# Four tokens on each partition, one batch on each 32 partitions, heads in two halves, in an RWKV attention with a soft mixture of experts

## The chip, the cores and the metric

One core of one Trainium2 chip. The metric is the time of one execution in microseconds of the device, the median of several runs. A run called slow here is over 1.5% above the fastest run of the same kernel; ratios use the other runs alone. A profile shows one execution. TensorE multiplies matrices, VectorE and ScalarE work element by element, GpSimd does too and also issues the DMA of the weights; SyncE issues the other DMA transfers.

## The reference

```python
# r, k, v: [B=4, H=8, S=768, D=48]   w (decay), u (bonus): [8, 48]   float32
for t in range(S):
    cur   = einsum('bhd,bhe->bhde', u * k[t], v[t])
    y[t]  = einsum('bhd,bhde->bhe', r[t], state + cur)
    state = w * state + einsum('bhd,bhe->bhde', k[t], v[t])
x = y.transpose(0, 2, 1, 3).reshape(3072, 384)          # tokens x model
logits = x @ phi                                        # phi: [384, 32], 8 experts of 4 slots
d = softmax(logits, over tokens); c = softmax(logits, over slots)
slot_in  = d.T @ x
slot_out = relu(slot_in[e] @ w1[e]) @ w2[e]             # per expert, F = 1024
return c @ slot_out                                     # [3072, 384]
```

Both kernels work in chunks of 128 tokens: within a chunk the scores k·r are masked by order and multiplied with v ("intra"), what came before is a state of 48 x 48 per head ("inter"), and decay is put into r and k beforehand by tables `W_n` and `W_k`. The loop has 12 steps in either kernel, of 256 tokens x 384 columns before and of 512 tokens x 192 columns after. Routing (transposes, logits, exponentials, dispatch sums) runs a step or two behind. Then come the expert matmuls and an output stage that writes 4.7 MB.

## The kernel before

A step is 256 tokens of one batch, two tokens on each of 128 partitions; all eight heads at once. So a chunk lies on 64 partitions, and a step's two chunks follow each other through one state.

```python
    def load(n):                                  # three transfers of 393 KB a step, 384-byte pieces
        b, i = divmod(n, nSb)
        for x, src in ((1, k), (0, r), (2, v)):
            nc.sync.dma_start(out=t[:].rearrange("p h j d -> p h (j d)"),
                              in_=src[b, :, i * TS:(i + 1) * TS, :].rearrange("h (p j) d -> p h (j d)", j=J))
    ...
    # att(n, j): 16 score matmuls (32 a step), 64x64 tiles; then two masking multiplies on VectorE
    nc.tensor.matmul(at_p[a][g * HF:(g + 1) * HF, q, :], kT[sl, q, g, j, :], rT[sl, q, g, :, :]...,
                     tile_position=(a * 64, g * HF))
    ...
        for n in range(nS):                       # cut: routing, loads, products
            att(n, 0)
            disp(n - 2, s_now); trans(n + 1, "rr")
            att(n, 1)
            r_copy(n + 1, 0); kur(n + 1, 0)
            y_open(n); inter(n, 0); state(n, 0); st_next(n, 0)
            r_copy(n + 1, 1); kur(n + 1, 1); v_cast(n + 1); trans(n + 1, "kk")
            xt(n - 1)
            inter(n, 1); state(n, 1); diag(n + 1); st_next(n, 1)
            intra(n); x_copy(n); lg(n - 1); expo(n - 1)
            load_w(W_AT[n])                       # one 768 KB weight transfer a step
```

Note the order: the masked scores of `att` are used by `intra` only at the end of the step, after all the state work.

The softmax here doesn't subtract the row's maximum and nothing guards it: scores larger than these inputs give would overflow.

## Time and profile before

| | kernel before |
|---|---|
| median, range | 137.83 us at first (3 runs), later rounds 135.7 to 137.8 |
| profiled run | span 137.7 us, a slow run |
| first masking multiply | 13.0 us |
| first to twelfth step | 83.9 us, 7.62 a step |
| last masking to expert matmuls, experts, output | 13.4, 11.8, 15.7 us |
| TensorE instructions | 3,454 (1,727 matmuls and as many weight loads) |

```profile
q8 instruction: 13, 0.21, 0.6%
...
PE 39%; DVE 26%; ACT 19%; issue 5%; DMA 5%; POOL 0%; DVEq 0%; ACTq 0%; POOLq 0%
```

"issue" is time in which an engine waits for nothing that the profile shows.

### The profile page before, as it was taken

The numbers are of one execution on the slowest core, as the hardware profiler recorded it, in microseconds if no ns is written. First come the engines' busy times: TensorE is split into PE (matmuls) and PEld (weight loads), VectorE is DVE, ScalarE is ACT, GpSimd is POOL, SyncE is SP. The second block draws the span as 40 slices with busy tenths as digits, with TensorE's granted clock in tenths as the row PEclk, the third lists the DMA queues.
The fourth block names the chain that finished last, engine by engine and source line by source line (L and its number), as shares of the span: only waits on it lengthen the run. The fifth ranks groups of instructions, "written<-read, shape, count | busy, mean of one in ns | idle before, by whom it ended". The sixth has DMA issues, their size and how long they took to land.

```text
span 137.7 us, 4106 instructions
## 1 busy us (share of the span) xinstructions
PE 98.7 (72%) x1727; PEld 67.7 (49%) x1727; DVE 98.0 (71%) x195; ACT 76.8 (56%) x130; POOL 78.6 (57%) x63
## 2 busy tenths in 40 slices
PE   0836897584889977795899859695788799958100
PEld 0325575463668665674578645574456444522000
DVE  6699998998896898789986878998833322078510
ACT  4839574949582776849573675949104212038510
POOL 5009999999999996295595959997520000000000
PEclk9999999999855699869757977999755557999755
DMA  2999999999999999999999999899999995009994
GB/s 32 318 321 321 321 328 302 214 277 212 282 210 310 212 274 205 258 213 222 200 283 166 201 306 212 152 186 205 203 204 204 205 202 91 5 0 402 406 407 161
DMA packets 51351, 31.78 MB, mean 231 GB/s; under 512 B 38386, under 2 KB 46836, under 8 KB 51332
## 3 DMA queue, kind: packets, MB, share of 16 engines
q0 software_dynamic: 11600, 12.63, 55.4%
q1 hardware_dynamic: 39316, 18.88, 47.7%
q8 instruction: 13, 0.21, 0.6%
q10 hardware_dynamic: 416, 0.00, 0.2%
q14 instruction: 6, 0.05, 0.1%
HBM read 39.38 MB, written 4.72 MB: 320 GB/s over the span
## 4 chain that ended last, share of the span: by engine, by line
PE 39%; DVE 26%; ACT 19%; issue 5%; DMA 5%; POOL 0%; DVEq 0%; ACTq 0%; POOLq 0%
DVE at_s L292 14%; PE at_p L287 7%; ACT t_kk L272 5%; DMA out_dram<-o_s 5%; ACT v_bf L219 4%; DVE k_l L238 4%; PE h_p L552 4%; PE t_p L269 4%; PE s_p L332 4%; ACT xt_s L381 3%; PE xl_p L379 3%; PE so_p L578 3%; ACT rp L232 2%; PE y_p L314 2%; DVE dv L256 2%
## 5 line engine op out<-in xcount | busy, mean ns | idle before, releaser
L292 DVE TENSOR_TENSOR at_s<-at_p,mask 128x512 bf16<-128x512 f32 x48 | 30.9, 685 | 8.4 <-PE at_p L287 8.3
L209 POOL TENSOR_TENSOR rr<-r_l,W_n 128x768 bf16<-128x768 f32 x11 | 20.3, 1847 | 17.7 <-DMA r_l<-in_r_dram 17.6
L212 POOL TENSOR_TENSOR k_l<-k_l,u_rep 128x768 f32<-128x768 f32 x11 | 19.9, 1811 | 0.9
L211 POOL TENSOR_TENSOR kk<-k_l,W_k 128x768 bf16<-128x768 f32 x11 | 20.0, 1814 | 0.0
L232 ACT COPY rp<-r_l 128x384 f32<-128x384 f32 x23 | 11.2, 487 | 12.6 <-DVE k_l L238 12.4
L287 PE MATMUL at_p<-t_rr,t_kk 64*64 64x128 bf16 x384 | 15.0, 258 | 3.9 <-DVE at_s L292 2.7
L170 POOL DMA_DIRECT2D w_all<-in_moe_w_dram x19 | 15.6, 831 | 2.6 <-DMA w_all<-in_moe_w_dram 2.6
L272 ACT COPY t_rr<-t_p 128x1024 bf16<-128x1024 bf16 x11 | 11.1, 1012 | 10.2 <-PE t_p L269 10.1
L272 ACT COPY t_kk<-t_p 128x1024 bf16<-128x1024 bf16 x12 | 12.1, 1005 | 2.2 <-PE t_p L269 2.1
L238 DVE TENSOR_TENSOR k_l<-k_l,rp 128x384 f32<-128x384 f32 x23 | 12.6, 549 | 0.7
L287 PEld LDWEIGHTS <-t_kk 64*64 64x64 bf16 x384 | 9.1, 126 | 7.8 <-issue 6.2
L332 PE MATMUL s_p<-v_bf,kk 64*128 64x96 bf16 x160 | 12.8, 234 | 0.0
L256 DVE TENSOR_TENSOR dv<-v_bf,rp 128x768 bf16<-128x768 bf16 x12 | 11.4, 953 | 1.5 <-ACT t_kk L272 0.5
L341 DVE TENSOR_TENSOR st<-s_p,wm 128x384 bf16<-128x384 f32 x20 | 11.0, 552 | 2.1 <-PE s_p L332 2.0
L332 PEld LDWEIGHTS <-kk 64*128 64x128 bf16 x160 | 9.3, 110 | 5.6 <-issue 5.6
L249 DVE TENSOR_REDUCE rp<-k_l 128x16 f32<-128x768 f32 x12 | 11.5, 958 | 0.3
L381 ACT COPY xt_s<-xl_p 128x768 bf16<-128x768 bf16 x11 | 8.8, 799 | 4.1 <-PE xl_p L379 4.1
L269 PE MATMUL t_p<-ident,kk 128*128 128x128 bf16 x96 | 9.1, 250 | 2.6 <-DVE kk L205 2.6
L365 ACT CAST x_t<-y_p 128x768 bf16<-128x768 f32 x11 | 8.9, 806 | 3.0 <-PE y_p L354 2.9
L615 ACT ACTIVATE o_s<-o_p,rsum_r 128x384 f32<-128x384 f32 x12 | 6.4, 583 | 6.4 <-PE o_p L607 4.2
L219 ACT CAST v_bf<-v_l 128x768 bf16<-128x768 f32 x12 | 9.9, 828 | 0.0
L354 PE MATMUL y_p<-v_bf,at_s 64*128 64x48 bf16 x384 | 9.6, 192 | 0.0
(105 smaller groups left out, 175.4 us busy)
## 6 DMA issues: line engine op xcount, KB each, us to landing
w_all<-in_moe_w_dram POOLq DMA_DIRECT2D x15, 768.0 KB, 10.1
k_l<-in_k_dram SPq DMA_DIRECT2D x12, 384.0 KB, 6.4
r_l<-in_r_dram SPq DMA_DIRECT2D x12, 384.0 KB, 5.9
v_l<-in_v_dram SPq DMA_DIRECT2D x12, 384.0 KB, 8.9
out_dram<-o_s SPq DMA_DIRECT2D x11, 384.0 KB, 4.2
w_all<-in_moe_w_dram POOLq DMA_DIRECT2D x4, 192.0 KB, 20.8
out_dram<-o_s SPq DMA_DIRECT2D x2, 192.0 KB, 1.9
phi_f<-in_moe_phi_dram POOLq DMA_DIRECT2D x1, 48.0 KB, 4.8
```

The costliest lines, as they stand in the source:

```text
L170: nc.gpsimd.dma_start(out=dst, in_=src)
L209: nc.gpsimd.tensor_mul(rr[:, :, :, 0:D], jh(r_l), W_n[:])
L211: nc.gpsimd.tensor_mul(kk[:, :, :, 0:D], jh(k_l), W_k[:])
L212: nc.gpsimd.tensor_mul(ku, ku, u_b)
L219: nc.scalar.copy(v_bf[:], jh(loads[n][2]))
L238: nc.vector.tensor_mul(s["ku"][:, j, :, :], s["ku"][:, j, :, :], s["rps"][j][:])
L256: nc.vector.tensor_mul(dv[:], s["v"][:], d[:, :, :, None].to_broadcast([P, J, H, D]))
L269: nc.tensor.transpose(t_p[:, q, :, j, :], s[nm][:, j, 2 * q:2 * q + 2, :].rearrange("p h d -> p (h d)"), ident[:])
L272: nc.scalar.copy(t_s[:], t_p[:])
L287: nc.tensor.matmul(at_p[a][g * HF:(g + 1) * HF, q, :], kT[sl, q, g, j, :], rT[sl, q, g, :, :].rearrange("p j c -> p (j c)"), start=True, s ...
L292: nc.vector.tensor_mul(s["at"][:, a, j, :, :], at_p[a][:], mask[:, j, None, :].to_broadcast([P, nP, P]))
L332: nc.tensor.matmul(s_p[:, q * D2:(q + 1) * D2], s["kk"][sl, j, 2 * q:2 * q + 2, :].rearrange("p h d -> p (h d)"), s["v"][sl, j, 2 * q:2 * ...
```

## The change

The intent: 768-byte pieces in the loads instead of 384, 6 KB rows in the stores instead of 3, state chains of four batches side by side, and dispatch sums that stay in PSUM instead of being added by VectorE. A step is now 128 tokens of all four batches and half of the heads: batch b lies on partitions 32b to 32b+31 with four tokens on each. Therefore score, intra and state matmuls work on tiles of 32 rows or columns, twice or four times as many, and each load or store is four transfers of 32 partitions, since the batches' rows are not evenly spaced in memory.

```diff
-    J = 2
-    HF = P // J
+    J = 4
+    PB = P // J
+    nS = 2 * nI
+    Hh = H // 2
@@ load
-            nc.sync.dma_start(out=t[:].rearrange("p h j d -> p h (j d)"),
-                              in_=src[b, :, i * TS:(i + 1) * TS, :].rearrange("h (p j) d -> p h (j d)", j=J))
+            for b in (0, 2, 1, 3):
+                nc.sync.dma_start(
+                    out=loads[n][x][b * PB:(b + 1) * PB, :, :, :].rearrange("p h j d -> p h (j d)"),
+                    in_=src[b, hq * Hh:(hq + 1) * Hh, i * C:(i + 1) * C, :].rearrange("h (p j) d -> p h (j d)", j=J))
@@ states: [128, 4 batches, 2 head pairs, 96], cleared at the start
+    for pair in st_t:
+        for t in pair:
+            nc.gpsimd.memset(t[:], 0.0)
@@ att: 64 matmuls a step in two batches of 32
-                        nc.tensor.matmul(at_p[a][g * HF:(g + 1) * HF, q, :], kT[sl, q, g, j, :], ...
-                                         tile_position=(a * 64, g * HF), ...)
+                            nc.tensor.matmul(at_p[a][b * PB:(b + 1) * PB, x, q, :],
+                                             kT[sl, q, b, j * PB:(j + 1) * PB], rT[sl, q, b, :],
+                                             tile_position=(a * 64, b * PB), ...)
@@ state: 64 small matmuls a step instead of 16, into the free columns of y's banks
+                            nc.tensor.matmul(s["y"][a * 64:(a + 1) * 64, b % 2, o:o + D], s["kk"][sl, j, 2 * q + a, :],
+                                             s["v"][sl, j, 2 * q + a, :], tile_position=(b * PB, a * 64), ...)
@@ the loop
-            y_open(n); inter(n, 0); state(n, 0); st_next(n, 0)
+            y_open(n, 0); inter(n, 0); intra(n, 0); state(n, 0); st_next(n, 0)
 ...
-            inter(n, 1); state(n, 1); diag(n + 1); st_next(n, 1)
-            intra(n); x_copy(n); lg(n - 1); expo(n - 1)
+            xt(n - 2); trans(n + 1, "kk"); lg(n - 2); expo(n - 2)
+            y_open(n, 1); inter(n, 1); intra(n, 1); state(n, 1)
+            dsum(n + 1); dmul(n + 1); st_next(n, 1); x_copy(n)
@@ dispatch sums: accumulated over the whole loop in one PSUM tile d_p; VectorE's add is gone
-            nc.vector.tensor_add(un_a[:], un_a[:], s_p[:, 0:w])
@@ output: two transfers of halves, then whole tiles, each in four parts of 32 partitions
-                nc.sync.dma_start(out=out_ap[i], in_=o_s[:])
+                    for b in (0, 2, 1, 3):
+                        nc.sync.dma_start(out=out_ap[b, i][:, lo * Dm:(j + 1) * Dm], in_=o_s[b * PB:(b + 1) * PB, ...])
```

## The prediction

> **What bounds the kernel now.** I read the page first: the rows of 40 slices (3.44 us each) for stages, the groups for the price of one instruction. Then the chain that ended last in order of time, then the busy time by step (a step runs from its first masking multiply on VectorE, line 292, to the next one's), and the timeline at both ends. The page:
>
> ```profile
> DVE  6699998998896898789986878998833322078510
> PEclk9999999999855699869757977999755557999755
> DMA  2999999999999999999999999899999995009994
> GB/s 32 318 321 321 321 328 302 214 277 212 282 210 310 212 274 205 258 213 222 200 283 166 201 306 212 152 186 205 203 204 204 205 202 91 5 0 402 406 407 161
> ...
> L292 DVE TENSOR_TENSOR at_s<-at_p,mask 128x512 bf16<-128x512 f32 x48 | 30.9, 685 | 8.4 <-PE at_p L287 8.3
> L332 PE MATMUL s_p<-v_bf,kk 64*128 64x96 bf16 x160 | 12.8, 234 | 0.0
> L341 DVE TENSOR_TENSOR st<-s_p,wm 128x384 bf16<-128x384 f32 x20 | 11.0, 552 | 2.1 <-PE s_p L332 2.0
> ```
>
> The DMA engines look full until about 112 us. With only the 384-byte r/k/v packets in flight (slices 1 to 5) they move about 320 GB/s; with only weights (slices 27 to 32) they write 204, and as the cast halves the bytes they read 408; the 3 KB output rows go at 405. So the loads pay a fifth for small packets: 14.16 MB takes 44 us at 320 and would take 35 at 405. But the chain has no load or weight transfer in it. At full clock one step of it is:
>
> ```profile
> 27.61 1.29 DVE at_s L292 x2
> 28.94 0.46 PE at_p L287 x15
> 29.40 1.28 DVE at_s L292 x2
> 30.68 0.47 DVE k_l L238
> 31.20 0.39 issue
> 31.59 0.83 ACT v_bf L219
> 32.42 0.91 ACT t_kk L272
> 33.33 0.71 ACT xt_s L381
> 34.40 0.40 PE at_p L287 x16
> 34.80 1.29 DVE at_s L292 x2
> ```
>
> 7.19 us from 27.61 to 34.80: VectorE masks twice with a TensorE batch between, then multiplies k by r, which frees the PSUM bank that ScalarE refills; three ScalarE copies follow, and the last holds TensorE's routing matmuls, which stand ahead of the next attention batch. By step (columns: stretch, length, then PE, PEld, DVE, ACT, POOL busy, granted clock, DMA, GB/s):
>
> ```profile
> 27.61:34.80 7.19, 4.82 (x121) 3.79 (x122) 6.17 (x11) 5.08 (x9) 7.09 (x6) 1.00 1.13 245
> 34.80:43.50 8.70, 7.63 (x133) 5.99 (x133) 6.95 (x13) 5.47 (x10) 8.58 (x7) 0.61 1.14 261
> 65.59:74.58 8.99, 8.29 (x135) 6.38 (x136) 6.79 (x13) 5.49 (x10) 6.27 (x4) 0.62 1.13 227
> ```
>
> At full clock VectorE is 86% busy and TensorE 67%; at clock 0.61 TensorE is 88 to 92% busy and the step takes 8.7 to 9.0 us. So two bounds alternate: the VectorE-ScalarE loop at full clock, TensorE when throttled. The first masking starts at 13.0 us, the twelfth step's at 96.9 (7.62 us a step), the expert matmuls at 110.3, the output stage at 122.0.
>
> **What the Trainium skill says.** (1) "DMA: Bandwidth & Descriptors", Specifications, asks for at least 512 B for line rate; the trace agrees (320 GB/s at 384 B against 405 at 3 KB). (2) "SBUF — State Buffer", Door 1: partitions 0 to 31 reach 8 of the 16 ports (189 GB/s measured there at 1 MiB), and a second DMA on the other half brought only 6%. The new loads and stores each cover 32 partitions. Every large transfer of this trace covers 128, so no run here shows it yet. (3) "TensorE: Matmul & The Clock Gate", Back-to-back issue gap, puts small matmuls at some 25 ns each. This trace differs: 30 weight loads of the local attention (L354, two row groups in turn) lie in 0.53 us, 15 ns apart after taking off one load's 0.09, and 16 of the score matmuls' (L287) in 0.26 us, 11 ns apart. I use 15 and 11. (4) "TensorEngine Tiling (Array Packing)", Key Properties: changing the tiling mode drains TensorE. The new step changes it more often (32-row tiles beside 64- and 128-row ones); the trace has no row for a drain, so I leave it out of the sum.
>
> **The change part by part.** Still 12 steps with the same number of elements, so the large VectorE, ScalarE and GpSimd instructions keep their shapes.
>
> Loads: 768 B. If they went at 400 GB/s, DMA work drops 9 us. As the chain has no transfer in it, this by itself buys about 0. GpSimd's waits for r (17.6 us, 7.7 of them before the first) go, but what it makes is used a step later.
>
> VectorE in a step: the dispatch add goes (278 ns). The state update turns from 2 instructions of 384 elements (552 ns) to 4 of 192. From 128 elements at 278 and 384 at 552: 1.07 ns an element plus 141, so 347 each. 4 x 347 - 2 x 552 - 278 = 0.0 us. It was already 86% busy; nothing is won.
>
> TensorE in a step: scores 32 to 64 matmuls, at 11 ns +0.35 us; local attention 32 to 64, at 15 ns +0.48; state 16 at some 37 ns to 64 at 11, +0.1; the state's identity 2 of 384 columns to 8 of 96 in two column halves, -0.15; y's opening 4 to 16, +0.1; row sums 4 to 16 in a third of the steps, +0.05. Sum +0.9 us on 4.8 at full clock, +1.5 at clock 0.6. All in all some 3,300 matmuls instead of 1,727.
>
> Waits: within a step the second half no longer waits for the first half's state (PE for st 2.0 us, DVE for s_p 1.1 us, over the whole loop). But the masked scores are now consumed directly: local attention and state of the first half (64 matmuls, 0.85 us and some 0.2 of latency) come straight after the second masking, and the state update stands on VectorE ahead of the second r-k multiply. The new chain after the second masking: multiply 0.47, r copy 0.48, v cast 0.82, routing copy 0.73, routing matmuls 0.2, then TensorE's second half ahead of the next scores (opening 0.16, inter-chunk 0.24, local 0.5, state 0.4), scores 0.6: 4.6 us. VectorE alone: 0.47, wait to 1.05, two updates 0.6, 0.45, sum 0.9, product 0.9, wait for the second state, 0.6: about 4.8. Then masking 1.29, a gap of 0.6 for 32 scores with nothing to fill it (the dispatch add filled it before), masking 1.28: 7.9 to 8.0 us against 7.2. In four steps the routing transposes also wait for the reciprocal behind that VectorE queue: +0.9. At clock 0.6 the same list gives 9.6 against 8.7 to 9.0. So +0.6 to +1.0 a step; 11 steps, +9 us if the clock is granted as now.
>
> Start: decay tables grow from 4 exponentials of 384 to 4 of 192 on ScalarE (about 0.33 each) and 3 of 768 (0.83), each behind a VectorE multiply of 768 (0.95). Two more mask builds (0.84) make VectorE free at about 6.2. Then 0.95 + 0.56 + 0.95 + three products 2.85 + 0.95 = 12.5; the last exponential holds ScalarE to 13.3; two r copies to 14.4; two transposed copies to 16.4; scores to 17.0. Before, 13.0: +4 us.
>
> End of the loop: the second head half must finish before the last two routings, which then run together; the last accumulations skip the adds (-1 us), but 16-matmul row sums, two fills and the second half's matmuls at clock 0.55 return it: 0. Experts: 0. Output: same bytes, 6 KB rows, first store after two tiles instead of one (+0.5), 28 issues instead of 13: 0 to +2.
>
> Sum: 137.8 + 4 + 9 + 0 + 1 = 151.8, all waits taken as I listed them.
>
> **Rivals.** (a) **The new order runs at VectorE's floor.** Busy parts without waits (2.57 masking, 1.0, 0.9, 0.9, 1.2) and the gap of 0.6 make 7.2 us; if TensorE's smaller tiles also draw less throttling (8.7 to 9.0 steps vanish), the loop gives 7.3 a step, -3.5 us, and with the start +4 all ends at 138, or 134 if half the start can be hidden. For it: the independent state chains leave much slack, the first half's matmuls fill TensorE's former waits (xl_p for xt_s, 7.8 us), and somebody balanced the start carefully. Against it: VectorE has no less work. (b) **Loads were the hidden bound**: the DMA share is full until the experts start, so shorter transfers let all move up; then up to -5 us, 132. Against it: no transfer in the chain, GpSimd's products ready some 2 us before use at 90 us. (c) **Ports bind**: 32-partition transfers at about 218 GB/s (the page's 8-port asymptote) make the loads 65 us instead of 44, and 4.7 MB of output 22 instead of 12: 155 to 160. The issue order 0, 2, 1, 3 alternates the halves, which speaks against the full loss.
>
> **Range and chances.** My sum is 152 and its floor 138. Hand-made chains tend to count waits in full that overlap, so I take about half of the loop's 9 and three quarters of the start: 137.8 + 4 + 3 + 0 = 144.8, and lower it to 144 for (a) and (b). Range 133 ((b), or (a) with a shorter start) to 153 (the full sum). Chances: faster 0.20 (needs (a) or (b)), same 0.20 ((a) with the start unpaid), slower 0.60.
>
> **What would show it.** Right: first masking near 16 to 17 us instead of 13.0; steps of about 7.9 at full clock; DVE busy in a step unchanged; the state rows four times as many; TensorE's matmul count near 3,300; the DMA row no longer full, or GB/s above 320 in the first slices. Wrong: steps at or under 7.2 us, a start under 14 us, the throttled slices gone, or GB/s near 200 in the loads-only slices with GpSimd waiting for r (rival c). The output slices' GB/s (405 now) decide the last term.

## The result

184.99 us (183.83 to 187.55, 5 runs) against 135.72 (135.2 to 137.9, 5 runs) on the same chip: the ratio is 1.362, 95% interval 1.353 to 1.370. A ratio here is the mean time of one kernel's fast runs over that of the other's of the same rounds, so not quite the ratio of the medians. The result is right. The predicted 144 and the range of 133 to 153 were missed by 41 and 32 us.

Where the 48.1 us between the two profiled runs (137.7 and 185.8 us, both slow ones) lie:

| stage | before | after | difference | predicted |
|---|---|---|---|---|
| start to first masking | 13.0 | 21.1 | +8.0 | +4 |
| first to twelfth step | 83.9 (7.62 a step) | 121.5 (11.04) | +37.6 | +9 in the full sum |
| last masking to expert matmuls | 13.4 | 13.3 | -0.1 | 0 |
| expert matmuls | 11.8 | 9.3 | -2.4 | 0 |
| output | 15.7 | 20.6 | +5.0 | +1 |

The page of the changed kernel, rows of slices (4.6 us each), instruction queue, chain:

```profile
PEclk9999999999999999999999999999999999999555
DMA  4777769999969598798989879979998000009985
GB/s 99 213 206 209 205 170 182 254 245 196 236 132 247 141 182 226 142 234 170 216 224 160 187 107 212 195 127 202 204 204 130 4 0 4 0 4 212 324 308 174
...
q8 instruction: 25, 0.41, 0.9%
...
PE 48%; DVE 16%; SPq 13%; issue 10%; ACT 5%; DMA 3%; DVEq 0%; ACTq 0%
```

Four things are to be seen. The loads-only slices 2 to 5 move 205 to 213 GB/s instead of 320, though the pieces doubled. TensorE's program has 25 packets instead of 13 (6,570 instructions, 3,285 matmuls; the prediction's count of 3,300 was right). The share of TensorE in the chain rose from 39 to 48% of a longer span, and "issue" from 5 to 10%, 18.6 us. And the clock row is a trap, of which more below. (SPq, 13%, is SyncE issuing transfers. 18 us of it are 41 issues of loads in a row, from 1.8 to 21.2 us; they come into the chain over one wait of ScalarE for r, 0.23 us long, at 23.2 us, so they do not set the start. The rest are stores at the end.) The groups:

```profile
L297 DVE TENSOR_TENSOR at_s<-at_p,mask 128x512 bf16<-128x512 f32 x48 | 30.9, 686 | 19.9 <-PE at_p L292 19.7
L209 POOL TENSOR_TENSOR kk<-k_l,W_k 128x768 bf16<-128x768 f32 x11 | 19.9, 1810 | 32.8 <-PE y_p L349 25.2
L360 DVE TENSOR_TENSOR st<-y_p,w_pd 64x192 bf16<-64x192 f32 x40 | 14.2, 355 | 24.9 <-PE y_p L349 24.6
```

VectorE's masking, 685 ns each before, takes the same, but waits 19.7 us for TensorE instead of 8.3; the state updates take 355 ns (347 were predicted) and wait 24.6 us for TensorE instead of 2.0. GpSimd, which ran short of r before, now waits for TensorE to give its buffers back. So VectorE does what was predicted and waits; TensorE is late. One step of the chain (start, length, what):

```profile
93.91 1.30 DVE at_s L297 x2
95.25 0.63 PE at_p L292 x27
96.17 0.43 PE y_p L327 x4
96.60 0.50 issue
97.47 0.75 PE y_p L373 x32
98.22 0.56 PE y_p L349 x22
98.78 0.77 PE xl_p L405 x6
99.62 0.81 ACT xt_s L410
...
101.84 0.75 PE y_p L373 x32
102.59 0.59 PE y_p L349 x22
```

The step is 10.05 us long (the next masking starts at 103.96). Scores (L292), inter (L327), intra (L373), state (L349), routing transposes (L405), then after ScalarE's copy the same list for the second half: TensorE's batches stand one behind the other in the chain, where the kernel before had VectorE and ScalarE in it.

**The clock.** The row PEclk shows 9 all through the loop, and a mean of 0.96. In the trace the first record of a granted clock comes at 154.5 us; time without a record is printed as full speed. The same eight transposes tell the truth. In the kernel before (weight loads of TensorE; start, busy time), once in a stretch recorded at full clock and once, after 36.7 us, in one recorded at half:

```profile
35.08 0.45 PEld L269 LDWEIGHTS <-rr 128*128 128x128 bf16 x8
...
37.79 0.77 PEld L269 LDWEIGHTS <-kk 128*128 128x128 bf16 x8
```

and in the changed kernel, in every step of the loop:

```profile
72.40 0.77 PEld L272 LDWEIGHTS <-rr 128*128 128x128 bf16 x8
```

0.77 us is the half clock's duration. So TensorE ran at half rate from start to the experts, where the kernel before had full clock recorded in 53 of the 84 us of its loop. (The experts, with full-array work before them, then had full clock, which is their -2.4 us.)

**Stops.** In the chain above "issue" stands for 0.50 us at 96.60. The largest such stops are these (timeline; in brackets the idle time ahead):

```profile
39.10 0.52 PE L292 MATMUL at_p<-t_rr,t_kk 64*32 64x128 bf16 x22 [2.03 <-issue]
```

TensorE stood for 2.03 us in the middle of a batch of equal score matmuls whose inputs had all been there for long. Counting TensorE's instructions in order of their start, the stops of the loop over 0.3 us that have no other cause lie at one place: number 193 of every 256. There are nine of them, 14.0 us together, counted from the start of the instruction before to the start of the late one (in some 11 of the 14 us TensorE is idle by the timeline); in the kernel before none reaches 0.3 us. The packet of the instruction queue (16 KB, 256 instructions) that belongs to this stop started at 36.36 us, 3.1 us after TensorE had passed the same place of the block before, and took 1.36 us.

**The start.** VectorE and GpSimd, before and after:

```profile
1.69 0.34 DVE L112 CAST col_f<-col_i 128x128 f32<-128x128 int32 x1
```

```profile
2.31 3.72 DVE L115 CAST col_f<-col_i 128x128 f32<-128x128 int32 x1
3.15 2.80 POOL L141 MEMSET st<- 128x768 bf16 x4
```

The same cast took 3.72 us instead of 0.34. It ended at 6.03, just after GpSimd's last clear of the new state buffers (5.95). The Trainium skill ("SBUF — State Buffer", Who interferes with whom) says that casts of VectorE in a two-port mode and GpSimd's instructions exclude each other for a whole instruction; the cast ending with the clears agrees with it, though its record begins 0.84 us before the first clear, which stays unexplained. The run st_late below tests it.

### The profile page after: what moved, and what is told of

It reads as the page before. It is cut to its first block, busy times and chain, and to the rows that moved or that the text cites. A ratio compares the mean times of both kernels' runs of the same rounds, so it can differ in the third digit from the quotient of the medians.

```text
span 185.8 us, 7461 instructions
## 1 busy us (share of the span) xinstructions
PE 130.7 (70%) x3285; PEld 92.1 (50%) x3285; DVE 106.2 (57%) x201; ACT 80.2 (43%) x131; POOL 83.1 (45%) x74
## 4 chain that ended last, share of the span: by engine, by line
PE 48%; DVE 16%; SPq 13%; issue 10%; ACT 5%; DMA 3%; DVEq 0%; ACTq 0%
SPq L73 10%; PE y_p L373 9%; DVE at_s L297 8%; PE at_p L292 6%; PE y_p L349 6%; PE xl_p L405 5%; PE y_p L327 4%; DVE st L360 4%; ACT xt_s L410 3%; PE y_p L314 3%; PE y_p L333 3%; SPq L647 3%; PE t_p L272 2%; PE so_p L607 2%; PE xl_p L425 2%
## 5 line engine op out<-in xcount | busy, mean ns | idle before, releaser
L297 DVE TENSOR_TENSOR at_s<-at_p,mask 128x512 bf16<-128x512 f32 x48 | 30.9, 686 | 19.9 <-PE at_p L292 19.7
L292 PE MATMUL at_p<-t_rr,t_kk 64*32 64x128 bf16 x768 | 19.8, 302 | 17.1 <-issue 8.3
L360 DVE TENSOR_TENSOR st<-y_p,w_pd 64x192 bf16<-64x192 f32 x40 | 14.2, 355 | 24.9 <-PE y_p L349 24.6
L213 POOL TENSOR_TENSOR rr<-r_l,W_n 128x768 bf16<-128x768 f32 x11 | 20.3, 1844 | 11.8 <-DMA r_l<-in_r_dram 7.1
L373 PE MATMUL y_p<-v_bf,at_s 32*128 32x48 bf16 x768 | 21.8, 210 | 1.6 <-DVE at_s L297 1.1
L292 PEld LDWEIGHTS <-t_kk 64*32 64x32 bf16 x768 | 10.1, 118 | 24.1 <-issue 18.2
L373 PEld LDWEIGHTS <-at_s 32*128 32x128 bf16 x768 | 17.2, 112 | 7.1 <-DVE at_s L297 2.3
L385 ACT CAST x_t<-y_p 128x768 bf16<-128x768 f32 x10 | 8.0, 798 | 24.8 <-DVE st L360 22.6
L272 PE MATMUL t_p<-ident,kk 128*128 128x128 bf16 x96 | 12.6, 312 | 5.9 <-DVE kk L209 5.9
L272 PEld LDWEIGHTS <-kk 128*128 128x128 bf16 x96 | 10.4, 147 | 7.2 <-DVE kk L209 7.1
L275 ACT COPY t_rr<-t_p 128x1024 bf16<-128x1024 bf16 x11 | 11.1, 1013 | 5.9 <-PE t_p L272 5.9
L349 PE MATMUL y_p<-v_bf,kk 32*64 32x48 bf16 x640 | 12.8, 225 | 0.0
L405 PE MATMUL xl_p<-ident,x_t 128*128 128x128 bf16 x66 | 8.9, 307 | 5.3 <-DVE rsum_r L474 5.3
```

The lines of the kernel that those rows point to most:

```text
L213: eng.tensor_mul(rr[:, :, :, 0:D], jh(r_l), W_n[:, hq, :, :, :])
L272: nc.tensor.transpose(t_v[:, q, :, j, :], s[nm][:, j, 2 * q:2 * q + 2, :].rearrange("p h d -> p (h d)"), ident[:])
L275: nc.scalar.copy(t_s[:].rearrange("x q b c -> x (q b c)"), t_p[:].rearrange("x q j c -> x (q j c)"))
L292: nc.tensor.matmul(at_p[a][b * PB:(b + 1) * PB, x, q, :], kT[sl, q, b, j * PB:(j + 1) * PB], rT[sl, q, b, :], start=True, stop=True, tile_ ...
L297: nc.vector.tensor_mul(s["at"][:, a, 2 * ph:2 * ph + 2, :, :], at_p[a][:], mask[:, 2 * ph:2 * ph + 2, None, :].to_broadcast([P, 2, Qh, P]))
L349: nc.tensor.matmul(s["y"][a * 64:(a + 1) * 64, b % 2, o:o + D], s["kk"][sl, j, 2 * q + a, :], s["v"][sl, j, 2 * q + a, :], start=False, st ...
```

## The experiments

The theories: **A**, TensorE runs out of instructions, because there are twice as many and they are fetched late. **B**, the half clock. **C**, the order: TensorE's work now lies in the chain. **D**, transfers in four parts: their issue, or their 32 partitions. 17 kernels ran. "Mean step" is from the first masking multiply of the first step to that of the twelfth, divided by 11; "stops" are those at place 193 of 256, over 20 us after the start. All in microseconds.

| run | median | ratio to before | first masking | mean step | stops | output |
|---|---|---|---|---|---|---|
| before | 135.7 to 137.8 | 1 | 13.0 | 7.62 | about 0 | 15.7 |
| the change | 184.99 | 1.362 | 21.1 | 11.04 | 14.0 | 20.6 |
| warm_burst | 185.02 | 1.364 | 21.1 | 10.99 | 14.1 | 22.1 |
| warm_kept | 188.09 | 1.385 | 20.9 | 11.27 | 13.2 | 20.8 |
| old_split | 164.05 | 1.197 | 13.0 | 9.91 | 14.3 | 15.7 |
| new_half | 171.91 | 1.255 | 21.0 | 9.51 | about 0 | 22.8 |
| new_quiet | 176.57 | 1.291 | 21.1 | 10.03 | 2.2 | 20.9 |
| st_late | 185.27 | 1.352 | 16.9 | 11.47 | 18.3 | 20.5 |
| quiet_late | 174.11 | 1.275 | 16.9 | 10.15 | 3.2 | 21.2 |
| quiet_late_warm | 170.70 | 1.238 | 16.7 | 10.00 | 3.4 | 21.0 |
| quiet_late_warm2 | 168.84 | 1.222 | 16.7 | 9.91 | 3.7 | 21.0 |
| quiet_late_group | 169.94 | 1.237 | 16.9 | 9.77 | 4.0 | 20.9 |
| old_32p | 167.28 | 1.222 | 13.0 | 9.25 | about 0 | 25.8 |
| old_heads | 157.48 | 1.147 | 13.0 | 9.40 | about 0 | 15.8 |
| new_wide | 282.34 | 2.052 | 19.8 | 16.88 | about 0 | 51.9 |
| old_heat | 140.38 | 1.023 | 13.0 | 8.34 | about 0 | 15.7 |
| new_repaired | 184.25 | 1.362 | 16.9 | 10.67 | 15.8 | 20.6 |

The intervals of the ratios reach at most 1.3% to either side, 1.8% for new_repaired, whose profile caught its fastest run (182.1). Profiles of before, the change, warm_burst, old_split, st_late and old_heat are of slow runs, the others of fast ones; fast runs of the kernel before are some 2 us shorter than the profiled one in all. The runs come from several chips, each with the kernel before measured beside it, so small differences between runs are better read from the ratios.

**ham_forms and dma_forms: the single costs.** Two small programs that do not compute the reference. The first sends streams of 700 to 900 matmuls of one shape (150 of the full array), idle time between, and after each stream eight full-array matmuls as a probe of the clock.

```diff
+    for form, count in ((st, 900), (intra32, 700), (sc32, 900), (intra64, 700), (sc64, 800), (full, 150)):
+        ...                                   # VectorE work for some 20 us, TensorE idle
+        for i in range(count):
+            form(t, i)                        # shapes of the change, then of the kernel before
+        probe(t)                              # 8 matmuls, 128x128, N = 128
```

> TensorE alone, output zeros on purpose (wrong). Six streams, each after some 13 us of idle and each followed by 8 full 128x128 matmuls of 128 columns as a probe: 900 of the changed state form (32 rows x 64 columns, N 48), 700 of its local attention (32x128, N 48), 900 of its scores (64x32, N 128), 700 of the old local attention (64x128, N 48), 800 of the old scores (64x64, N 128), 150 full ones (128x128, N 128). Theory A (small tiles do not count as work for the clock): the probe after the 32-row forms shows 107 ns between weight loads (half clock), after the full form 53 to 56 ns; the old forms somewhere between. Theory B (what keeps the clock down is idle time, not tile size): every probe shows 53 to 56 ns, as each stream is 10 us or longer without a break. If the streams of the small forms show breaks every 256 instructions, that is the instruction fetch by itself.

Measured (timeline):

```profile
30.51 1.91 PE L31 MATMUL y<-t_st 32*64 32x48 bf16 x128 [1.55 <-issue]
...
46.04 0.77 PEld L63 LDWEIGHTS <-t_st 128*128 128x128 bf16 x8
...
153.22 0.45 PEld L63 LDWEIGHTS <-t_intra 128*128 128x128 bf16 x8
```

Two results. The probe after 900 state matmuls of 32 x 64 still ran at half clock (0.77), as did those after the change's intra (32 x 128) and score (64 x 32) tiles; after the old kernel's tiles (64 x 128, 64 x 64) and after the full array it ran at full clock (0.45). The change's streams were no shorter (19 to 24 us from first to last against 17 to 21) at much the same mean spacing (26 to 27 ns a matmul against 25 to 26), so it was the shape, not the time or the number of instructions, that decided whether TensorE's work released the clock. The records agree: full clock begins 6.0 and 4.1 us into the two streams of old tiles, and no record begins within the three of the change. (The first one, 3.4 us of full clock at 121.6, follows the third stream and its probe; why, is not shown.) And with no other transfer on the chip, a stream of state matmuls stands still after every 128 of them (128 matmuls and 128 weight loads, 256 instructions) for 1.3 to 2.1 us: one block every 3.45 to 4.0 us, though the 256 instructions of the state shape run in 1.9.

The second program moves 4.7 MB in each form of transfer.

```diff
+    whole(8, 2)                               # 384-byte pieces, 128 partitions
+    whole(4, 4)                               # 768-byte pieces, 128 partitions
+    quarters((0, 2, 1, 3))                    # 768-byte pieces, four transfers of 32 partitions
+    quarters((0, 1, 2, 3))
+    quarters((0, 2, 1, 3), two=True)          # every second one issued by ScalarE
+    ...                                       # then stores: 3 KB whole, 6 KB in quarters, two orders
```

> Transfers alone, output zeros on purpose (wrong). 4.7 MB each time, from the SP queue: 128 partitions with 384-byte pieces; 128 partitions with 768-byte pieces; 32 partitions with 768-byte pieces in order 0,2,1,3; the same in order 0,1,2,3; the same from SP and ACT in turn; then stores: 128 partitions with 3 KB rows; 32 partitions with 6 KB rows in order 0,2,1,3; in order 0,1,2,3. Theory A (issue binds the loads: 0.46 us an issue of 98 KB is 212 GB/s): 320, then 370 to 410, then 205 to 215 for both orders on one queue, and clearly more (300 or over) from two queues. Theory B (ports bind[...]): about 200 from two queues as well, and order 0,1,2,3 no better than 0,2,1,3. Stores: 405 for 128 partitions; 32 partitions 300 to 330 in order 0,2,1,3, and under 250 in order 0,1,2,3 if ports bind.

Measured, from first to last packet: 254, 289, 203, 201 and 227 GB/s for the loads; 392, 301 and 250 for the stores (3 KB whole, quarters in the order 0, 2, 1, 3, quarters in order). The loads in whole transfers stayed under the expectation (320 and 370 to 410). A quarter's issue takes SyncE 0.46 us, and 98 KB in 0.46 us is 212 GB/s: the issue alone caps the quarters on one engine. With two issuing engines they reach 227, neither the 300 of theory A nor the 200 of B, so something else stands close behind; the ports may be it, but that was not separated. The stores depend on the order, as they would if the ports had a part.

**warm_burst and warm_kept: theory B by itself.** The changed kernel with idle full-array matmuls (into free columns of the dispatch bank, results unused): 32 before the loop, or these and eight in each step.

```diff
+        def heat(count):
+            for _ in range(count):
+                nc.tensor.matmul(d_p[:, 128:512], ident[:], mask[...][:, 0:384], ...)
         trans(0, "kk")  ...  trans(0, "rr")
+        heat(16)                              # at two places before the loop
@@ warm_kept only, in the loop
             trans(n + 1, "rr")
+            heat(4)
             trans(n + 1, "kk")
+            heat(4)
```

> The changed kernel with 32 idle full matmuls (128x128 by 384 columns, into unused columns of a bank) ahead of the loop, 16 before and 16 after the first transposes, where TensorE idles; 5 us of them at half clock. If TensorE's half clock is what makes the steps long (transposes 8 in 0.77 us of weight loads instead of 0.45): the first transposes of the loop run at 0.45, and if the loop's own work then keeps the clock up, steps fall from 11.0 to 8.5 to 9.5 us and the time from 185 to 160 to 170; if the loop cannot hold the clock, only the first one or two steps gain, under 4 us. If the clock does not matter: 185 within 1%.

> As warm_burst, and 8 more such idle matmuls in every step at the two places where TensorE waits (4 after each transposed half). They cost 8 x 0.16 = 1.3 us of TensorE time a step at full clock, part of it inside waits. If the clock is the cause and small tiles do not hold it: steps at full clock throughout, 9 us or less, time 155 to 168. If the clock does not matter: 185 to 200, since the step only gets more TensorE work.

warm_burst: the clock was full from 12 to 19 us, then recorded at 0.5 to 152 us: the loop cannot hold what it is given. No gain. warm_kept held it for about half of the loop (mean 0.78) and was 3 us slower. So clock is not the whole cause; but each group of four idle matmuls stood in the chain with 1.28 us at half clock, and 24.5 us of the chain (38 to 101 us) are now waits for loads of k, v and r, which the change's loop, after its first step, does not have. So this run does not free B of guilt either.

**old_split: theory A in the kernel before.** The same arithmetic, layout, transfers and order, with score, intra and state matmuls cut along their columns.

```diff
-                        nc.tensor.matmul(at_p[a][..., q, :], kT[sl, q, g, j, :], rT[sl, q, g, :, :]..., ...)
+                        for z in range(2):
+                            nc.tensor.matmul(at_p[a][..., q, z * HF:(z + 1) * HF], kT[sl, q, g, j, :], rT[sl, q, g, z, :], ...)
@@ likewise intra in two halves of 24 columns, state in four of 24
```

> The kernel before with its score, local-attention and state matmuls cut along their columns, so that the same arithmetic, layout, loads and chain take about 5,950 TensorE instructions (matmuls and weight loads) instead of 3,454; the change has 6,570. Theory A (TensorE runs out of instructions: it stops where a new block of 256 begins): stops longer than 0.3 us appear at one place in every block of 256, 8 us of them or more in sum (0.3 in the kernel before), the mean step goes from 7.6 to 9.5 to 11 us, the time to 155 to 175 us. Theory C (the change is slow because of its longer chain of dependent work, not because of the number of instructions): some 104 more matmuls in a step at 11 to 15 ns each, 1.4 us of TensorE work partly in its gaps: step 7.9 to 8.6, time 138 to 147, no such stops. Theory B (half clock): if the narrower matmuls lower the granted clock, the record shows 0.5 over most of the loop.

Measured: 164 us, 13 stops with 14.3 us at the same place of each block. One of them:

```profile
114.67 0.13 PEld L315 LDWEIGHTS <-t_rr 128*128 128x128 bf16 x2 [1.98 <-issue]
```

A holds, and in a kernel that has none of the change's other parts. The narrower matmuls also lost the clock (recorded 0.5 from 39 us on but for two short stretches; this is a slow run, clock 0.63 in the mean, but the fast ones show 0.70 to 0.76 against 0.81 to 0.87 in the kernel before). Their tiles have the rows and columns of the old ones, so the tile is not all that counts. And so the 2.3 us a step are not stops alone: 1.3 are. (One more piece of its chain, 9.6 us at 34 us, is a load of v.) Three of its steps met no stop and took 7.8 us, at half clock (their eight transposes take 0.77 us) and with nearly twice the instructions: the old order hides the slower TensorE nearly wholly.

**new_half: A from the other side.** The change with pairs of batches or heads merged into one matmul: 4,394 TensorE instructions. Its output is wrong, which doesn't matter for the time.

```diff
-                    for b in range(B):                      # scores, M = 32
+                    for b in (0, 2):                        # M = 64, two batches' rows at once
-            for q ... for a in range(2): for j ...          # intra, N = 48
+            for q ... for j ...                             # N = 96, one head's scores for both
-                    for a in range(2): ...                  # state, M = 64
+                    ...                                     # M = 128
```

> The change with half of its score, local-attention and state matmuls (pairs of batches or heads merged into one; the result is wrong on purpose), everything else as it is: about 4,300 TensorE instructions instead of 6,570, the same chain of VectorE, ScalarE and GpSimd work, loads and stores. Theory A: the stops at block borders fall from 14 us to under 4 and the mean step from 11.0 to 7.8 to 8.8; time 150 to 160. Theory C: the step stays at 10 us or more, time 172 to 182. The scores have 64x64 tiles here, so the clock may also be granted; the kept-warm run showed that alone to be worth nothing.

The stops are gone, as A says, but 9.51 us a step is between the two expectations: stops are a part of the loss, and not the larger one. Two parts of its chain, at 85 and 89 us, are now waits for loads of r and v. The clock stayed at half (the eight transposes of r take 0.77 us in every step, scores on 64x64 tiles or not). And a step without row sums takes 9.19 us with 335 TensorE instructions in it (86.72 to 95.91), against 9.69 with 527 in quiet_late_group below: once the stops are gone, the number of matmuls matters little.

**new_quiet: why the fetch is late.** One expert's weights loaded and used eight times. Its output is wrong, which doesn't matter for the time.

```diff
-    w1_all = wts.tile([P, E, nM, F], bf, name="w1_all")
+    w1_all = wts.tile([P, 1, nM, F], bf, name="w1_all")
@@ likewise w2_all; the list of loads has one expert, every use reads index 0
```

> The change with one expert's weights loaded and used eight times (wrong on purpose): 1.6 MB instead of 12.6 MB of weights written, nothing else changed in the loop. If the DMA traffic is what makes the fetch of instructions late: stops at block borders from 14 us to under 6, mean step under 10.3, time 172 to 178. If the traffic has no part in it (the instructions are fetched one block ahead at a fixed pace, and the chain does the rest): stops 11 us or more, mean step 10.7 to 11.2, time 181 to 186.

As the first expectation said: the stops fall from 14.0 to 2.2 us, both of the remaining ones before 43 us, while these weights were still coming in, and the loop loses 11 us. After 43 us the instruction packets start at most 1.5 us after TensorE passes place 193, where in the change they started 1.2 to 4.5 us after. (In the kernel before they start up to 3.4 us after it as well, but there a block lasts 6.1 us or more, and nothing waits.) So the step needs a block about every 4.6 us (9.7 us with 2.1 blocks), and it comes too late when its packet stands behind 768 KB of weights. That it stands in the same engines' queues is inferred from this; no view shows a queue's order.

**st_late: the start.** VectorE clears the states itself, one in each of the first four steps.

```diff
-    for pair in st_t:
-        for t in pair:
-            nc.gpsimd.memset(t[:], 0.0)
@@ loop
             att(n, 0)
+            if n < 4:
+                nc.vector.memset(st_t[n % 2][1 - n // 2][:], 0.0)
```

> The change with the four clears of the state buffers taken from GpSimd at the start and done by VectorE one in each of the first four steps, after the masking. If the clears hold VectorE's first instructions up (one took 3.72 us instead of 0.34 while they ran): first masking at 17.7 to 18.6 us instead of 21.05, time 181.5 to 183. If the start is bound by something else (decay rows, loads, exponentials): first masking 20.5 or later, time 184 to 185.

```profile
2.31 0.21 DVE L115 CAST col_f<-col_i 128x128 f32<-128x128 int32 x1
```

The cast is short again and the first masking comes at 16.9 us, 4.2 earlier: the clears were the cause of these 4.2, and what is left over the kernel before, 3.8 us, is the +4 of the prediction. The time did not move: the stops grew to 18.3 us, mostly in the fifth and sixth steps, and the loop took it all back.

**quiet_late, and the clock again.** new_quiet and st_late together; then with idle matmuls as in warm_kept; then with three after the transposes of r and three before the first intra, where TensorE waits for a masking.

```diff
@@ quiet_late_warm2
             trans(n + 1, "rr")
-            heat(4)
+            heat(3)
             ...
             inter(n, 0)
+            heat(3)
             intra(n, 0)
```

> The change with one expert's weights (wrong on purpose, as in new_quiet) and the clears of the state buffers moved into the first four steps (as in st_late). In st_late the first masking came 4.2 us earlier, but the stops at block borders grew from 14.0 to 18.3 us and took it all back. If that was the late fetch of instructions behind the weights' traffic, the gain stays here: first masking 16.9, stops under 3.5 us, mean step 9.9 to 10.2, time 171.8 to 173.5. If something else fixes when the loop ends, 175.5 to 177 as in new_quiet.

> quiet_late with the idle 384-column matmuls of warm_kept (16 twice before the loop, 4 twice in each step), which keep the clock granted for at least half of the loop. With the stops gone, the half clock (theory B) can show: if it makes the remaining 10.0 us of a step, the mean step falls to 7.9 to 8.7 and the time to 150 to 160; the prediction's list said 7.9 to 8.0 at full clock and 9.6 at 0.6. If the order of the work makes it at any clock (theory C), the step stays at 9.4 or more, time 166 or more.

> quiet_late with idle matmuls as in quiet_late_warm, but three where TensorE waits for the first masking and three where it waits for the second. If half clock makes the step (B): with the clock held in most of the loop the steps of 9.68 us become 8.0 to 8.7, mean 8.3 to 9.1, time 152 to 163. If the order makes it (C): mean 9.5 or more, time 167 or more. If the clock isn't held (record 0.5), nothing is settled.

quiet_late kept 2.5 of the 4.2 us, a little less than expected. Its steps alternate between 9.68 and 11.25. By the letter both warm runs came out for theory C (means of 10.00 and 9.91). But the records show full clock in only 63 and 48% of their loops, the four idle matmuls of the first stood in the chain with 1.28 us again, and in both the chain also waits for loads (for v at 51 and 67 us in the first, for v at 67 and r at 86 us in the second). So single steps say more: the fifth of the first run, all of it recorded at full clock, and a late one of the second (columns: stretch, length, then PE, PEld, DVE, ACT, POOL busy, granted clock, DMA, GB/s):

```profile
56.93:66.56 9.63, 7.72 (x287) 5.71 (x285) 6.97 (x14) 5.38 (x9) 5.45 (x4) 1.00 0.60 159
...
107.62:116.62 9.00, 8.24 (x276) 5.94 (x273) 6.93 (x13) 5.18 (x8) 2.95 (x2) 0.87 0.02 4
```

The fifth step takes 9.63 us with its eight idle matmuls, where quiet_late's takes 11.25 at half clock with none: the half clock costs this step 1.6 us at least, if the idle matmuls only add to it. The late step, at a clock of 0.87 and without DMA traffic, takes 9.0 us with three idle matmuls, 0.96 us, in its chain; quiet_late's takes 9.68 at half clock with none. Less the idle work it would have been about 8.0, an estimate from these two numbers. Another estimate comes out near it: the TensorE pieces of the chain at half clock, each against the same piece at full clock in the other runs (scores 0.63 and 0.45, intra 0.58 and 0.42, 0.75 and 0.51, state 0.56 and 0.37, 0.59 and 0.41, transposes 0.77 and 0.51), save 1.2 us together, so 9.68 becomes 8.5. No run held the clock through the whole loop, so the mean itself was not measured.

**quiet_late_group: every second step.** Row sums in free columns of the dispatch bank, so that the next transposes of the routing do not share a bank with them.

```diff
-            rs_p = lt_of.pop(i)[:, P:P + 2 * J].bitcast(f32)
+            rs_p = d_p[:, (nM + 1) * ES + i * J:(nM + 1) * ES + (i + 1) * J]
```

> quiet_late with the row sums of the routing in free columns of the dispatch bank, so that the routing transposes needn't wait for their reciprocal on VectorE. The steps of 11.25 us (every second one) become 9.7 to 10.3, mean 9.5 to 9.8, time 167 to 171 against 174.1. If another wait takes its place at once, steps of 10.9 or more, time 173 to 175.

As expected: the steps of 11.25 become 9.91, 4.2 us in all. The rest is a nearly even 9.7, in which TensorE is busy 9.4 us (9.37 in the step from 86.28 to 95.97): at half clock it has hardly any room left. But only two thirds of the chain of this step are TensorE's; masking and state updates of VectorE (2.0 us) and ScalarE's copy (0.8 us) stand in it too. So TensorE's load and the order of the work give about the same length here, and which of the two sets it is not shown.

**old_32p and old_heads: theory D in the kernel before.** Loads in four parts, by partitions (and the stores too) or by heads.

```diff
@@ old_32p
+            for z in (0, 2, 1, 3):
+                nc.sync.dma_start(out=t[z * 32:(z + 1) * 32, ...], in_=src[b, :, i * TS + z * 64:i * TS + (z + 1) * 64, :]...)
@@ old_heads
+            for z in range(4):
+                nc.sync.dma_start(out=t[:, 2 * z:2 * z + 2, :, :]..., in_=src[b, 2 * z:2 * z + 2, ...]...)
```

> The kernel before with each load and each store (but the first two) cut into four of 32 partitions, issued in the change's order 0, 2, 1, 3; packets stay 384 B and 3 KB. Theory D (transfers of 32 partitions and their issue): the loads-only slices move 190 to 215 GB/s instead of 320 and the output slices about 300 instead of 405. If the loads are hidden behind the work, the mean step stays 7.5 to 7.9 and only the output stage grows, 15.7 to 19 to 21 us: time 139 to 142. If slow loads reach the chain, the mean step passes 8.2 and the time 146.

> The kernel before with each load cut into four of two heads over all 128 partitions (98 KB each, as many issues as in old_32p; stores left whole). If the issue caps the loads (0.46 us each on the queue's engine, 98 KB / 0.463 us = 212 GB/s): loads-only slices 200 to 215 GB/s as in old_32p, mean step 8.9 to 9.4, time 155 to 162 (old_32p had 9.25 and 167, of which some 5 are stores). If the 32 partitions cap them (ports): slices 280 to 320, mean step 7.5 to 7.8, time 136 to 140.

I had expected the loads to stay hidden, and they did not: +30 us, 10 of them in the output stage, where the stores of 98 KB went at 208 to 212 GB/s instead of the 300 expected. old_heads, with the same number of transfers over all 128 partitions, has the same slow loop, 9.40 us a step:

```profile
GB/s 60 205 199 185 197 151 176 182 251 203 209 182 155 229 249 251 140 209 213 209 239 195 144 210 245 243 141 220 197 196 209 203 205 204 183 6 217 414 412 161
...
L211 POOL TENSOR_TENSOR rr<-r_l,W_n 128x768 bf16<-128x768 f32 x11 | 19.8, 1804 | 38.8 <-DMA r_l<-in_r_dram 30.3
```

(The first line is old_heads, the second the page of old_32p.) So for these loads, on one issuing engine, it is the number of issues and not the partitions. One issue of 98 KB takes 0.46 to 0.50 us of SyncE, and the loads-only slices fall from 320 to about 200 GB/s in both; GpSimd, which makes r ready, waits 30 us for r where it waited 17.6, and transfers are now in the chain: 42% of old_32p's (v 13%, weights 11%, k 10%, r 4%). The kernel before had its loads hidden, but with no room: loads and weights, 26.8 MB, then kept the DMA busy to 117 us, and in old_heads to 138.

**new_wide: the repair that cost 97 us.** The change with its loads by head over 128 partitions, and one transfer for each output tile.

```diff
-            for b in (0, 2, 1, 3):
+            for h in range(Hh):
                 nc.sync.dma_start(
-                    out=loads[n][x][b * PB:(b + 1) * PB, :, :, :]..., in_=src[b, hq * Hh:(hq + 1) * Hh, ...]...)
+                    out=loads[n][x][:, h, :, :]..., in_=src[:, hq * Hh + h, ...].rearrange("b (p j) d -> b p (j d)", j=J))
```

> The change with its loads cut by head over 128 partitions instead of by batch over 32 (12 issues of 98 KB a step as before, 768 B packets), and each output tile stored in one transfer of 128 partitions. Output stage: 20.7 us to 15.5 to 17 in either case. Loop: if issue caps the loads, slices stay at 205 to 215 GB/s, first masking 21.05 and mean step 11.0 as in the change, time 179 to 182. If ports cap them, slices of 260 or more and time 165 to 177.

```profile
DMA  2222226437282462927429274273999902222221
GB/s 51 93 93 93 96 93 140 110 100 151 92 167 84 120 130 92 166 77 147 96 95 157 83 144 97 94 154 84 194 207 204 181 7 70 106 107 106 106 108 67
```

Both expectations failed. 93 GB/s in the loads, 106 in the stores, with the DMA engines at two tenths: a quarter of them worked. The Trainium skill ("DMA: Bandwidth & Descriptors", Why a DMA increments its semaphore by 16 and not by 1) says that a transfer is spread over the largest number of engines up to 16 that divides the slowest dimension of both sides; here the memory side's slowest dimension is the four batches, so four engines, and both rows agree with it. So cutting by batch, as the change does, at least keeps all the engines at work.

**old_heat and new_repaired: can anything of it be used?**

```diff
@@ old_heat: the kernel before, from the third step on, after each of the two transposes
+                for _ in range(8):
+                    nc.tensor.matmul(sc[n]["s"][:, 384:512], ident[:], mask[:, 0, :], ...)
@@ new_repaired: the change with the edits of st_late and quiet_late_group, all weights
```

> The kernel before with eight idle full-array matmuls of 128 columns twice in each step from the third on, into the unused columns of the state's bank. If the half clock in some 45% of its loop comes from TensorE not being busy enough, those stretches vanish: the steps of 8.5 to 9.0 us become 7.4 to 7.6, time 131 to 134.5. If the grant is taken back whatever TensorE does, or because it does too much, the idle work only adds: time 136 to 141.

> The change with both repairs, correct and with all weights: clears in the first four steps, row sums in the dispatch bank. If the loop's length is set by its own chain plus stops that come at random: some 6 us off, time 177 to 180. If, as in st_late, shorter steps only meet the load stream and the late instruction fetch sooner (the load and weight stream of 26.8 MB ended at 138 us in the change, 4 us before the last step began), the gain is given back: time 182 to 186, stops of 16 us or more.

old_heat lost 2.3% (interval 1.3 to 3.3). Its profile is of a slow run: clock 0.87, with stretches at half clock left in the loop and the idle work in the chain with up to 1.0 us. (The half clock of the kernel before is on record for 24 of the 84 us of its loop, 28%, not the 45% of the expectation.) Its four fast runs show a clock of 0.93 to 0.95, against 0.81 to 0.87 in those of the kernel before; the half clock at the end of the program alone takes 0.05, so little may have been left in their loops. They were slower all the same: here the idle work cost more than the clock gave. new_repaired is correct and no faster than the change: its repairs saved 6.7 us without the weights' traffic (176.57 to 169.94; as ratios 1.291 to 1.237) and with it none that the interval shows. In its profile GpSimd waits 38 us for loads (14 in the change) and the stops are 15.8 us. (The weights' last packet ended at 143.3 us in the change, not at the 138 of the expectation.) No version beat the kernel before.

## Why the prediction was wrong

The direction was right (slower, at 0.6), and so was much of the working. The size was not: 48 us instead of 14 in the full sum.

- **VectorE's list.** Right: 355 ns for a state update (347 predicted), masking unchanged at 686, 6.9 us busy in a step as before. It waits instead, as the prediction's chain had it.
- **The start, +4.** The listed items gave +3.8 in st_late. What failed is that the list left out GpSimd: its clears held VectorE's cast up for 3.4 us, and without them the first masking came 4.2 us earlier; 3.8 and 4.2 make the +8.0.
- **The loop, +9.** The list at full clock said 7.9 to 8.0 us, at clock 0.6 it said 9.6. quiet_late measured 9.68 at half clock. (That this fits so well is in part luck: carried on from 0.6 to a clock of 0.5, the list's own two figures would give 10.4, an estimate.) The step that failed is its condition, "if the clock is granted as now". The change's tiles do not release the clock (ham_forms), so something like the second figure held in every step; what that costs I can only estimate, 1.2 to 1.7 us a step, 13 to 19 in all (the one step measured at full clock was 1.6 us shorter with idle work in it). The group steps' wait for the reciprocal, predicted at 0.9 in four steps (3.6 in all), was 1.3 in every second one, 4.2 us in all. The drain at a change of tiling mode, which the prediction left out of its sum, was separated by no run.
- **What the sum had no term for: the instruction stream.** 3,300 matmuls were counted, at 11 and 15 ns each. Those durations are about right inside a block, but with the weight loads they are 6,570 instructions, and a block of 256 came no faster than every 3.45 us in ham_forms, later beside the weights: 14.0 us of stops. The rates were read from bursts of 16 and 30, shorter than a block, which cannot show this.
- **Loads, "about 0".** It was argued that the chain has no transfer in it. Right for the kernel before, wrong as a licence: four times the issues make 98 KB / 0.46 us = 212 GB/s at most, and old_heads shows that this alone costs 20 us in a kernel that hid its loads. In the change this limit lies just under the others: where the work before it was shortened, in st_late and new_repaired, GpSimd waited 30 and 38 us for loads instead of 14, the stops grew, and the gain was given back.
- **Rival (c), ports, 155 to 160.** Its figure of 218 GB/s was nearly met (205 to 213), but the first cause is another: the issue, as old_heads shows over 128 partitions. Whether the ports would hold the loads at about the same rate, once two engines issue them (227), is not settled. The sign named for it, GB/s near 200 in the loads-only slices, came; it stood in the text and got too little weight.
- **Output, +1.** +5.0: the quarters of 6 KB rows reach 300 GB/s in the stores (slices of 308 and 324 against 402 to 407), with 28 issues.
- **Rivals (a) and (b)** failed: less throttling, faster loads. Both were the reverse of what came, so the step from 152 down to 144, taken for them and for waits that would overlap, went the wrong way.

The parts do not add up to one sum, since they overlap: loads in four parts beside the weights held a step at about 9.4 us (old_heads), the new order at half clock at 9.7 (quiet_late_group), and the stops come on top of whichever is last. What the runs leave of the loop's 37.6 us is: 11.1 that went with the weights' traffic (new_quiet), 4.2 with the row sums' bank (quiet_late_group), and some 22 for order and half clock together. How those divide stays open to the width of the estimates above, because no idle work was found that holds the clock without standing in the chain.

## What to carry to other kernels

Before splitting matmuls into smaller tiles, count TensorE's instructions, weight loads too, in blocks of 256 per step, and compare the time of a block with the fastest that a long stream shows, not with a burst's spacing. Before splitting a transfer, divide its bytes by the time of one issue: if that is below the rate it has now, the loads may stop being hidden. And a clock row without records says nothing; take the duration of one and the same instruction in both kernels.

## What the Trainium skill lacked or had wrong

- "TensorE: Matmul & The Clock Gate", Part 1, explains the throttle by how busy TensorE was, without saying that the matmul's shape counts: streams of 32 x 64, 32 x 128 and 64 x 32 tiles left the probe at 0.77 us for eight weight loads, streams of 64 x 64 and 64 x 128 brought it to 0.45.
- "Runtime: NRT & Kernel Launch", Instruction fetch mechanics, has the blocks of 16 KiB and 256 instructions, with which the packets here agree (25 for 6,570 TensorE instructions), but calls the cost of crossing from one to the next mostly hidden. It was not: long streams of small matmuls got a block every 3.45 to 4.0 us, 27 ns for a matmul with its weight load, with stops of 0.6 to 2.1 us; the change lost 14.0 us to such stops, up to 2.7 us each, beside the weights.
- "TensorE: Matmul & The Clock Gate", Back-to-back issue gap: its floor of some 25 ns does not hold within a block for small tiles in alternate rows: 128 state matmuls in 1.91 us are 15 ns each.
- "DMA: Bandwidth & Descriptors", Issuing engines are not separate DMA queues, calls the time to initiate usually small beside the transfer. Here it was 0.46 us for a transfer of 98 KB, which took all the loads to 200 GB/s, and a second issuing engine brought 227 instead of 203.
- "SBUF — State Buffer", "Can I just issue two DMAs to hit both halves?", says that transfers to the two halves serialize (+6%). The stores in quarters reached 301 GB/s when neighbours in the queue were on different halves and 250 in plain order, against 392 for whole tiles.
- "TensorE: Matmul & The Clock Gate", Part 1, says that single clock records are not to be fully trusted, but no page says that there may be no record at all for a loop at half clock: the profile's row counts such time as full speed and showed 0.96.
